# Two fused layer pairs on one core: separate q/k/v places for the first five chunks, a direct wo load, an instruction order planned from other costs, and down weights issued from GpSimd's queue

## The chip, the cores and the metric

The kernel runs on one core of a Trainium2 chip. The metric is device time in microseconds, as a median over runs of the whole program; the kernel before has 1096.06 (1095.94 to 1097.07, three runs). A separate profiled execution gives the trace from which all durations are read. TensorE does the matmuls, VectorE and ScalarE the elementwise work, GpSimd (POOL) set-up work, and SyncE (SP) issues the DMAs.

## The reference, cut to what matters

`x` is 2048 tokens by 576 channels. Attention has 32 heads of 18 channels, and each token looks at itself and at the tokens 2, 4, ... 14 before it.

```python
def A(x, wqkv, wo):                      # sliding, dilated attention
    q, k, v = split_heads(x @ wqkv)      # 576 -> 3 x 576
    idx = pos[:, None] - 2 * arange(8)   # 8 keys per token
    logits = sum_d(q * k[idx]) * Dh ** -0.5
    attn = softmax(where(idx >= 0, logits, -1e9))
    return merge_heads(sum_w(attn * v[idx])) @ wo
def B(x, w_gate, w_up, w_down):          # 576 -> 4608 -> 576
    return ((x @ w_gate) * (x @ w_up)) @ w_down

x = x + A(layernorm(x)); x = x + B(layernorm(x))
x = x + A(layernorm(x)); x = x + B(layernorm(x))
```

Both A layers share their weights, and so do both B layers.

## The kernel before, in words

**Chunks.** The tokens are cut into chunks, and a chunk goes through one A and one B before its x is kept in `xf`. The sequence `seq` holds 18 chunks, numbered j: for the first half of the tokens the first layer pair in chunks of 128, 128, 128, 128, 256 and 256 tokens (j = 0 to 5), then the second pair in four chunks of 256; then the second half of the tokens likewise in eight chunks of 256. A chunk needs the last 14 tokens of k and v of the chunk before it in its layer (the "halo").

**Attention of a chunk** (`attention`). `head` makes the layernorm: statistics on VectorE (L343, L344), rstd on ScalarE, nmr on VectorE (L352), and the normalized x on ScalarE (L358, with the last 64 channels a second time, L359). The transpose goes over TensorE (L369) and ScalarE (L372) for j below 5, by DMA (L362) otherwise. `project` multiplies with `wqkv` (L407) into the PSUM banks pg and pu, and ScalarE (for j = 0 partly VectorE) evacuates q, k and v into `qT`, `kT`, `vT` (L449 to L484). There are two sets of these places, and chunk j uses set j % 2: a projection can't be started before the chunk two before it has done its last product with v. Then VectorE multiplies q with shifted k (L503), adds (L507 to L512), TensorE sums over the channels (`Esel`, L518), VectorE and ScalarE do the softmax (L540 to L551). The weights of the softmax are spread to all channels: for j below 5 by TensorE (`Bsel`, L557) and copies (L447, L449), otherwise through DRAM, with one store (L567) and four loads `ab` (L570). VectorE multiplies with shifted v and adds up (L587, L602), in chunk 0 with TensorE adding (L591, L592). TensorE multiplies with `wo_p` (L614), VectorE adds x (L620), and a second `head` makes the input of B.

**B of a chunk** (`glu`). 36 slices of 128 hidden channels are done in units of 512 columns: gate and up by TensorE (L655, the last 64 channels as pairs of half matmuls, L666), ScalarE copies the gate out of PSUM (L677), VectorE multiplies (L678, `h`). After a phase of nine units (three for a chunk of 128 tokens), the "downs" multiply h with `wd` (L699, L700), and VectorE adds the sum to x (`settle`, L709, L714). Three PSUM pairs rotate among the units; a pair is free when its h is done.

**Down weights.** `load_wd` (L682) loads them in pieces of 288 KB into six buffers, issued by SyncE (324 loads). For a chunk of 256 tokens a phase has nine loads. They are recorded ahead of the downs of their phase, so the second load into a buffer waits for the landing of the first, and not for a down; the first three units of such a phase multiply with the weights of its last three. Both kernels do so.

**Start.** `wqkv` is loaded in five parts into `wraw`, and its columns are reordered by copies: columns t3 = 0 and 2 by VectorE (L292), 1 and 3 by ScalarE (L294). `setup_wo` loads wo into DRAM in the order of channels, then into `wo_p` (L320, L323). `setup_glu` loads gate and up in six slices; both stay in SBUF.

**Order.** Nothing is written out by hand. Every operation is recorded with an engine, a cost in ns, what it reads and writes, and a priority (`op`). `Plan.run` (L69) then simulates the engines with these costs: it takes again and again the operation that can start first, and emits it. The order so found is the order of each engine's instructions; the engines run in order, and so do the queues of SyncE and GpSimd. The PE work of B is one chain in fixed order (`bb`); matmuls of attention are put between.

Of the kernel before, what the change touches and what calls it, by code (L numbers as in the profile page):

```python
# [7 lines left out]
FP32 = mybir.dt.float32  # L8
# [7 lines left out]
class Op:  # L16
    __slots__ = ("eng", "cost", "fn", "deps", "order", "succ", "n", "prio", "idx", "hold", "free",
                 "lat", "margin", "ready", "end", "nbytes", "use", "pair", "need")


class Plan:
# [4 lines left out]
    LAT = {"PE": 250, "ACT": 130, "DVE": 110, "POOL": 150, "SP": 0}  # L26
# [6 lines left out]
    def op(self, eng, cost, fn, r=(), w=(), prio=1, after=None, hold=None, free=None, margin=0, nbytes=0, use=None,  # L33
           pair=None, need=None):
        o = Op()
        o.eng, o.cost, o.fn, o.prio, o.hold, o.free = eng, cost, fn, prio, hold, free
# [32 lines left out]
    def run(self, slots):  # L69
        clock = {e: 0.0 for e in self.LAT}  # L70
        dma = 0.0
# [3 lines left out]
        while cand:  # L75
            best = None
            for o in cand:
# [6 lines left out]
                if o.hold is not None:  # L84
                    f = free[o.hold]
                    if not f:
                        continue
                    t = max(t, min(f)[0])
                if o.pair is not None:
                    if len(free["unit"]) < len(o.pair):  # L90
                        continue
                    t = max(t, min(free["unit"])[0])
# [40 lines left out]
def kernel(  # L133
# [44 lines left out]
    wo_dram = dram.tile([D, D], BF16, name="wo_dram")  # L178
# [13 lines left out]
    xf = [sb(f"xf{i}", [P, NST, D], FP32) for i in range(NXS)]  # L192
# [9 lines left out]
    xnT_B = [sb(f"xnT_B{i}", [P, KT, CH]) for i in range(NXB)]  # L202
    qT_ = [sb(f"qT{i}", [P, KT, CH]) for i in range(2)]
    kT_ = [sb(f"kT{i}", [P, KT, HALO + CH]) for i in range(2)]
    vT_ = [sb(f"vT{i}", [P, KT, HALO + CH]) for i in range(2)]
    oT = sb("oT", [P, KT, CH])
    n_al = nlayers // 2
    halo_k = [sb(f"halo_k{i}", [P, KT, HALO]) for i in range(n_al)]
    halo_v = [sb(f"halo_v{i}", [P, KT, HALO]) for i in range(n_al)]
# [46 lines left out]
    def load_x(t0, nst):  # L256
        b, i0 = (t0 // 2) % 2, t0 % 2
        op("SP", 600, dma(xb[b][:, i0:i0 + nst, :], xv[:, t0:t0 + nst, :]), w=[f"xb{b}_{i}" for i in range(i0, i0 + nst)],
           nbytes=P * nst * D * 2, prio=1.5 if t0 else 0)
# [13 lines left out]
    def setup_b():  # L273
        def mk_zero():
            for t_ in qT_ + kT_ + vT_:
                nc.gpsimd.memset(t_[TL:P, KF, :], 0.0)
            for t_ in halo_k + halo_v:
                nc.gpsimd.memset(t_[:], 0.0)
        op("POOL", 1500, mk_zero, w=[f"{x}{t}{i}" for x in "qkv" for t in (4, "H") for i in range(2)] + [f"halo{x}{i}" for x in "kv" for i in range(n_al)])
        for k in range(KT):  # L280
            for t3 in (0, 1, 2, 3):
                if t3 < 3:
                    src = wraw[:, k, t3 * D:(t3 + 1) * D].rearrange("p (h d) -> p d h", h=H)[:, 0:16, :]
                    dst = wqkv[:, k, t3 * 512:(t3 + 1) * 512].rearrange("p (d h) -> p d h", h=H)
                    cost = (615, 1080)
                else:
                    src = wraw[:, k, :].rearrange("p (t h d) -> p t d h", t=3, h=H)[:, :, 16:18, :]
                    dst = wqkv[:, k, 3 * 512:3 * D].rearrange("p (t d h) -> p t d h", t=3, h=H)
                    cost = (280, 500)
                rk = [f"wraw{k}"] if k < KF else ["wrawt0", f"wrawt{TL}"]  # L290
                if t3 % 2 == 0:
                    op("DVE", cost[0], lambda dst=dst, src=src: nc.vector.tensor_copy(dst, src), r=rk, w=[f"wq{t3}_{k}"], prio=2)  # L292
                else:
# [10 lines left out]
        op("POOL", 9000, mk_sel, w=["sel"])  # L304
# [12 lines left out]
    def setup_wo():  # L317
        op("SP", 600, dma(wo_dram[:].rearrange("(d h) n -> h d n", h=H), A_wo.rearrange("(h d) n -> h d n", d=Dh)),
           w=["wod"], nbytes=D * D * 2, prio=2)
        op("SP", 600, lambda: nc.sync.dma_start(wo_p[:, 0:KF, :], wo_dram[0:KF * P, :].rearrange("(t p) n -> p t n", p=P)),  # L320
           r=["wod"], w=["wo0"], nbytes=KF * P * D * 2, prio=2)
        for r_ in (0, TL):
            op("SP", 600, lambda r_=r_: nc.sync.dma_start(wo_p[r_:r_ + TL, KF, :], wo_dram[KF * P:D, :]),  # L323
               r=["wod"], w=[f"wot{r_}"], nbytes=TL * D * 2, prio=2)
# [11 lines left out]
    def head(src, keys, nst, dst, key, prio, ab, on_pe, mg):  # L336

        mv, st, rstd, nmr, xn = mv_[ab], st_[ab], rstd_[ab], nmr_[ab], xn_[ab]
        for i in range(nst):
            def stats(i=i):  # L340
                xr = src(i).rearrange("p (a b) -> p a b", a=2)
                for a in range(2):
                    nc.vector.bn_stats(out=st[:, i, a, :], in_=xr[:, a, :])  # L343
                nc.vector.bn_aggr(out=mv[:, i, :], in_=st[:, i])  # L344
            op("DVE", 1070, stats, r=[keys[i]], w=[f"mv{ab}{i}"], prio=prio)
        mk = [f"mv{ab}{i}" for i in range(nst)]

        def rs():
            nc.scalar.activation(rstd[:, 0:nst], mv[:, 0:nst, 1], ACT.Ln, bias=eps_t[:])
            nc.scalar.activation(rstd[:, 0:nst], rstd[:, 0:nst], ACT.Exp, scale=-0.5)  # L350
        op("ACT", 490, rs, r=mk + ["eps"], w=[f"rstd{ab}"], prio=prio)
        op("DVE", 210, lambda: nc.vector.scalar_tensor_tensor(nmr[:, 0:nst], mv[:, 0:nst, 0], -1.0, rstd[:, 0:nst],  # L352
                                                              op0=ALU.mult, op1=ALU.mult),
           r=mk + [f"rstd{ab}"], w=[f"nmr{ab}"], prio=prio)
        for i in range(nst):
            def apply(i=i):
                x = src(i)
                nc.scalar.activation(xn[i][:, 0:D], x, ACT.Identity, bias=nmr[:, i:i + 1], scale=rstd[:, i:i + 1])  # L358
                nc.scalar.activation(xn[i][:, D:D + TL], x[:, KF * P:D], ACT.Identity, bias=nmr[:, i:i + 1], scale=rstd[:, i:i + 1])  # L359
            op("ACT", 1300, apply, r=[keys[i], f"nmr{ab}", f"rstd{ab}"], w=[f"xn{ab}{i}"], prio=prio)  # L360
            if not on_pe:
                op("SP", 900, lambda i=i: nc.sync.dma_start_transpose(out=dst[:, :, i * P:(i + 1) * P], in_=xn[i][:]),  # L362
                   r=[f"xn{ab}{i}"], w=[key + str(i)], prio=0, nbytes=P * KT * P * 2)
# [3 lines left out]
            def tr(i=i, b=b):  # L367
                for k in range(KT):
                    nc.tensor.transpose(bf(b())[:, k, :], xn[i][:, k * P:(k + 1) * P], ident[:])  # L369
            o = op("PE", 290, tr, r=[f"xn{ab}{i}", "ident"], prio=0, margin=mg, **b.take())  # L370
            pl.also(o, [key + str(i)])
            op("ACT", 700, lambda i=i, b=b: nc.scalar.copy(dst[:, :, i * P:(i + 1) * P], bf(b())), r=[b.key], w=[key + str(i)],  # L372
# [4 lines left out]

    def attention(j, la, t0, nst):
        fast = j == 0
        z = j % 2  # L380
        qT, kT, vT = qT_[z], kT_[z], vT_[z]
# [8 lines left out]
        xk = [f"xA{i}" for i in range(nst)]  # L390
        head(lambda i: xin[:, i0 + i, :], xin_k, nst, xnT_A, "xA", prio, 0, on_pe, mg)
        op("ACT", 250, lambda: nc.scalar.copy(kT[:, :, 0:HALO], halo_k[la][:]), r=[f"halok{la}"], w=[f"kH{z}"], prio=prio)
# [4 lines left out]
        def project(tag, au, bu, tl, ea, eb, dkeys):  # L397
# [7 lines left out]
            def mm(u, part, k, r_, start, stop):  # L405
                p_, e, c0, m = part
                nc.tensor.matmul(bank(p_, u)[0:m, e * n:(e + 1) * n], lhsT=wqkv[r_, k, c0:c0 + m], rhs=xnT_A[r_, k, 0:n],  # L407
# [387 lines left out]
```

## Time and profile before

| | |
|---|---|
| median of three runs | 1096.06 us |
| profiled execution | 1094.6 us |
| its span | 1092.5 us |
| VectorE busy, 200 to 600 us | 81% to 87% by 100 us |
| first gate matmul | at 43.20 us |
| DMA, 20 to 60 us, by 10 us | 319 to 347 GB/s |
| first load issued to its landing, down weights | median 3.4 us, 2.6 to 10.2 |

The span is one profiled execution from its first to its last instruction; 2.1 us of the profiled execution lie around it. A row of a timeline has the start, the length, the engine, the line of the kernel, the operation with output and inputs, and in brackets the idle time ahead of it with what ended it. PEld is TensorE's weight loading, which runs beside its matmuls. SPq is the issuing of DMAs on SyncE. A group's mean length can be longer than the pace of such operations in a row, since one begins before the last has quite ended.

### The profile page before, as it was taken

The numbers are of one execution on the slowest core, as the hardware profiler recorded it, in microseconds if no ns is written. First come the engines' busy times: TensorE is split into PE (matmuls) and PEld (weight loads), VectorE is DVE, ScalarE is ACT, GpSimd is POOL, SyncE is SP. The second block draws the span as 40 slices with busy tenths as digits, with TensorE's granted clock in tenths as the row PEclk, the third lists the DMA queues.
The fourth block names the chain that finished last, engine by engine and source line by source line (L and its number), as shares of the span: only waits on it lengthen the run. The fifth ranks groups of instructions, "written<-read, shape, count | busy, mean of one in ns | idle before, by whom it ended". The sixth has DMA issues, their size and how long they took to land.

```text
span 1092.5 us, 25296 instructions
## 1 busy us (share of the span) xinstructions
PE 1057.1 (97%) x10812; PEld 792.8 (73%) x10812; DVE 761.4 (70%) x1347; ACT 364.1 (33%) x768; POOL 5.9 (1%) x26
## 2 busy tenths in 40 slices
PE   5889999999999999999999899999999999999998
PEld 4668887777777777777767677777787777777775
DVE  6688889697979868798978563785757867322222
ACT  7435254432244443323342222314242232211111
POOL 2000000000000000000000000000000000000000
PEclk9899999999999999999999999999999999999999
DMA  8954563633333532535361434342333323333331
GB/s 261 336 155 119 172 200 98 183 110 97 95 99 102 147 84 74 135 112 155 99 168 24 122 99 122 92 121 56 117 106 122 107 72 121 105 96 109 116 110 55
DMA packets 146239, 133.17 MB, mean 122 GB/s; under 512 B 42000, under 2 KB 145488, under 8 KB 146128
## 3 DMA queue, kind: packets, MB, share of 16 engines
q1 hardware_dynamic: 146128, 131.57, 41.9%
q8 instruction: 84, 1.38, 0.5%
q14 instruction: 27, 0.22, 0.1%
HBM read 118.96 MB, written 4.73 MB: 113 GB/s over the span
## 4 chain that ended last, share of the span: by engine, by line
PE 88%; DVE 5%; DMA 4%; SPq 1%; issue 1%; ACT 1%; DVEq 0%; ACTq 0%
PE pu L655 21%; PE pg L655 21%; PE pg L699 12%; PE pu L699 10%; PE pg L666 6%; PE pg L407 6%; PE pu L407 4%; PE pa L614 3%; PE acct L700 3%; DMA a_dram<-s 2%; DMA ab<-a_dram 1%; SPq L570 1%; DMA wraw<-in_A_wqkv_dram 1%; DVE h L678 1%; DVE prod L503 1%
## 5 line engine op out<-in xcount | busy, mean ns | idle before, releaser
L677 ACT CAST g_sb<-pg 128x512 bf16<-128x512 f32 x288 | 158.9, 586 | 493.6 <-PE pu L666 359.7
L655 PE MATMUL pg<-xnT_B,wg 128*128 128x256 bf16 (+1 forms) x2592 | 301.1, 262 | 1.1 <-ACT xnT_B L372 1.1
L655 PE MATMUL pu<-xnT_B,wu 128*128 128x256 bf16 (+1 forms) x2592 | 301.9, 262 | 0.1
L678 DVE TENSOR_TENSOR h<-pu,g_sb 128x512 bf16<-128x512 f32 x288 | 193.3, 684 | 130.6 <-ACT g_sb L677 74.8
L655 PEld LDWEIGHTS <-wu 128*128 128x128 bf16 x2592 | 225.2, 98 | 40.1 <-issue 16.5
L655 PEld LDWEIGHTS <-wg 128*128 128x128 bf16 x2592 | 230.2, 98 | 28.9 <-issue 1.5
L699 PE MATMUL pg<-wd,h 128*128 128x512 bf16 x648 | 231.9, 382 | 0.0
L700 PE MATMUL acct<-wd,h 128*128 128x64 bf16 x1152 | 222.4, 193 | 0.0
L699 PEld LDWEIGHTS <-h 128*128 128x128 bf16 x1152 | 113.0, 98 | 130.5 <-issue 1.1
L699 PE MATMUL pu<-wd,h 128*128 128x512 bf16 x504 | 191.5, 380 | 0.9 <-DVE h L678 0.9
L587 DVE TENSOR_TENSOR prod<-vT,ab 128x1280 bf16<-128x1280 bf16 (+1 forms) x127 | 94.0, 741 | 47.1 <-DMA ab<-a_dram 46.0
L407 PEld LDWEIGHTS <-wqkv 128*128 128x128 bf16 (+1 forms) x1260 | 98.7, 99 | 25.6 <-issue 14.5
L700 PEld LDWEIGHTS <-h 128*128 128x128 bf16 x1152 | 113.1, 98 | 2.1 <-issue 1.1
L503 DVE TENSOR_TENSOR prod<-qT,kT 128x2560 bf16<-128x2560 bf16 (+1 forms) x72 | 95.7, 1332 | 22.4 <-ACT kT L449 21.9
L602 DVE TENSOR_TENSOR oT<-oT,prod 128x1280 bf16<-128x1280 bf16 (+1 forms) x119 | 90.8, 763 | 3.2
L666 PE MATMUL pu<-xnT_B,wgu_t 64*128 64x256 bf16 (+1 forms) x648 | 79.7, 259 | 4.2 <-DVE h L678 4.2
L407 PE MATMUL pg<-xnT_A,wqkv 128*128 128x256 bf16 (+3 forms) x650 | 79.7, 265 | 2.5 <-ACT xnT_A L372 1.6
L666 PE MATMUL pg<-xnT_B,wgu_t 64*128 64x256 bf16 (+1 forms) x648 | 79.8, 259 | 0.0
L407 PE MATMUL pu<-xnT_A,wqkv 128*128 128x256 bf16 (+3 forms) x610 | 77.2, 266 | 0.1
L709 DVE TENSOR_TENSOR xf<-pg,xf 128x512 f32<-128x512 f32 (+1 forms) x40 | 27.4, 684 | 66.3 <-PE pg L699 58.4
L666 PEld LDWEIGHTS <-wgu_t 64*128 64x128 bf16 x1296 | 50.3, 94 | 27.8 <-issue 22.6
L614 PE MATMUL pa<-wo_p,oT 128*128 128x288 bf16 x310 | 48.2, 286 | 2.5 <-DVE oT L602 1.8
(91 smaller groups left out, 614.0 us busy)
## 6 DMA issues: line engine op xcount, KB each, us to landing
wd<-in_B_w_down_dram SPq DMA_DIRECT2D x324, 288.0 KB, 3.4
ab<-a_dram SPq DMA_DIRECT2D x52, 128.0 KB, 2.7
wg<-in_B_w_gate_dram SPq DMA_DIRECT2D x6, 768.0 KB, 9.4
wu<-in_B_w_up_dram SPq DMA_DIRECT2D x6, 768.0 KB, 10.7
out_dram<-xf SPq DMA_DIRECT2D x8, 288.0 KB, 5.4
wraw<-in_A_wqkv_dram SPq DMA_DIRECT2D x4, 432.0 KB, 5.5
xb<-in_A_x_dram SPq DMA_DIRECT2D x6, 288.0 KB, 4.6
a_dram<-s SPq DMA_DIRECT2D x13, 128.0 KB, 2.2
```

The costliest lines, as they stand in the source:

```text
L407: nc.tensor.matmul(bank(p_, u)[0:m, e * n:(e + 1) * n], lhsT=wqkv[r_, k, c0:c0 + m], rhs=xnT_A[r_, k, 0:n], start=start, stop=stop, skip_g ...
L503: nc.vector.tensor_tensor(late["prod"][p_ % 2][:, :, :, 0:n], q2, k2, op=ALU.mult)
L587: nc.vector.tensor_tensor(js(dst), js(vT[:, :, o0:o0 + n]), abw, op=ALU.mult)
L602: op("DVE", 60 + 3 * n, lambda i_=i_: nc.vector.tensor_tensor(oT[:, :, 0:n], oT[:, :, 0:n], late["prod"][i_ % 2][:, 0, :, 0:n], op=ALU.add ...
L614: nc.tensor.matmul(b()[:, 0:HD], lhsT=oT[:, t, i * P:(i + 1) * P], rhs=wo_p[:, t, hh * HD:(hh + 1) * HD], start=(t == 0), stop=(t == KT - 1))
L655: nc.tensor.matmul(pt[:, e * n:(e + 1) * n], lhsT=w_[:, k, ft * P:(ft + 1) * P], rhs=xT[:, k, 0:n], start=(first and k == 0 and e == 0), s ...
L666: nc.tensor.matmul(ps[:, e * n:(e + 1) * n], lhsT=wgu_t[r_, ft * P:(ft + 1) * P], rhs=xT[r_, KF, 0:n], start=(first and e == 0), stop=not ...
L677: op("ACT", 590, lambda: nc.scalar.copy(g_sb[gs][:, 0:ul], pg[use["slot"]][:, 0:ul]), r=[f"wg_{j}_{u}"], w=[f"g{gs}"], prio=0)
L678: op("DVE", 690, lambda: nc.vector.tensor_tensor(hb[hs][:, 0:ul], pu[use["slot"]][:, 0:ul], g_sb[gs][:, 0:ul], op=ALU.mult), r=[f"wu_{j}_{ ...
L699: nc.tensor.matmul((pg, pu)[i][use["slot"]][:], lhsT=lhs, rhs=wt[:, e % 2, 0:512], start=first, stop=fin)
L700: nc.tensor.matmul(acct[:, i * TL:(i + 1) * TL], lhsT=lhs, rhs=wt[:, e % 2, 512:D], start=(first and i == 0), stop=fin, skip_group_check=True)
L709: op("DVE", 690, lambda i=i, dst=dst: nc.vector.tensor_tensor(dst[:, 0:512], (pg, pu)[i][use["slot"]][:], xs_f[:, i0 + i, 0:512], op=ALU.add),
```

## The change

- Chunks 0 to 4 get places of their own for q, k and v: the two sets are cut in halves for the four chunks of 128, and chunk 4 uses memory of `xf` (buffers 2 and 3) that is not needed yet. k and v lie in one tile, so that the halo takes one copy instead of two each way.
- Chunk 4's x is loaded a second time, early, into a part of `xf` (`xtmp`), and its first layernorm is recorded with chunk 3.
- wo goes from its input to `wo_p` directly, in six loads.
- A third of the copies that reorder `wqkv` goes to GpSimd; VectorE and ScalarE divide the others anew. GpSimd also clears the new places.
- For j below 5, L359 is left out and the transposes of the last 64 channels take their place (12 more on TensorE); for chunks of 128 tokens the softmax weights are spread in two copies instead of four.
- Nearly all costs in the recorded operations are different, most of them lower. The model of DMAs has a queue for GpSimd and some extra latency (`late`). Gate copies and h are marked `due`: an operation that isn't due is put off if it would delay one that is by more than a slack.
- All loads of down weights but the first six are issued by GpSimd.

In the built order the counts of matmuls by line are unchanged but for the 12 transposes. The projections of chunks 2 and 3 stand ahead of the first gate matmul, and chunk 4's stands in the first phase of chunk 0's B. SyncE issues 178 DMAs, transposes included, instead of 493, GpSimd 318 instead of none.

```diff
 class Plan:
-    LAT = {"PE": 250, "ACT": 130, "DVE": 110, "POOL": 150, "SP": 0}
+    LAT = {"PE": 250, "ACT": 150, "DVE": 150, "POOL": 150, "SP": 0}
...
+                if o.due and (o.eng not in urgent or key < urgent[o.eng][0]):
+                    urgent[o.eng] = (key, o)
+            o = best[1]
+            if not o.due and o.eng in urgent and urgent[o.eng][0][0] < best[0][0] + o.cost - SLACK[o.eng]:
+                best = urgent[o.eng]
...
-                dma = max(dma, o.end) + o.nbytes / 250.0
-                o.ready = dma + 2000
+                dma[o.eng] = max(dma[o.eng], o.end) + o.nbytes / (250.0 if o.eng == "SP" else 200.0)
+                o.ready = dma[o.eng] + 2000 + o.late
...
-                if t3 % 2 == 0:
+                if t3 == 0 or t3 == 3:
                     op("DVE", cost[0], lambda dst=dst, src=src: nc.vector.tensor_copy(dst, src), ...)
+                elif t3 == 2:
+                    op("POOL", 1000, lambda dst=dst, src=src: nc.gpsimd.tensor_copy(dst, src), ...)
...
     def setup_wo():
-        op("SP", 600, dma(wo_dram[:].rearrange("(d h) n -> h d n", h=H), A_wo.rearrange("(h d) n -> h d n", d=Dh)), ...)
-        op("SP", 600, lambda: nc.sync.dma_start(wo_p[:, 0:KF, :], wo_dram[0:KF * P, :].rearrange("(t p) n -> p t n", p=P)), ...)
+        wv_ = A_wo.rearrange("(h d) n -> h d n", d=Dh)
+        for dd in range(4):
+            op("SP", 470, dma(wo_p[32 * dd:32 * dd + 32, 0:KF, :], wv_[:, dd:16:4, :]), ...)
...
+    def place(j, nst):
+        if nst == 1:
+            z, h = j // 2, j % 2
+            return [2 * z + h], qT_[z][:, :, h * P:h * P + P], kv_[z][:, :, :, h * (HALO + P):(h + 1) * (HALO + P)], h * P
+        if j == 4:
+            return ["x"], q_x, kv_x, 0
+        z = (j + 1) % 2
+        return [2 * z, 2 * z + 1], qT_[z][:], kv_[z][:, :, :, 0:HALO + CH], 0
...
-        z = j % 2
-        qT, kT, vT = qT_[z], kT_[z], vT_[z]
+        zs, qT, kv, c0 = place(j, nst)
+        kT, vT = kv[:, 0], kv[:, 1]
...
-            op("ACT", 590, lambda: nc.scalar.copy(g_sb[gs][:, 0:ul], pg[use["slot"]][:, 0:ul]), ..., prio=0)
-            op("DVE", 690, lambda: nc.vector.tensor_tensor(hb[hs][:, 0:ul], ...), ..., prio=0, free="unit", use=use)
+            op("ACT", 490, lambda: nc.scalar.copy(g_sb[gs][:, 0:ul], pg[use["slot"]][:, 0:ul]), ..., prio=0, due=True)
+            op("DVE", 605, lambda: nc.vector.tensor_tensor(hb[hs][:, 0:ul], ...), ..., prio=0, due=True, free="unit", use=use)
...
-            op("SP", 550, dma(wd[b][:], wd_v[g]), ...)
+            first = wd_no["n"] <= NWD
+            eng, q = ("SP", nc.sync) if first else ("POOL", nc.gpsimd)
+            op(eng, 550 if first else 1100, lambda: q.dma_start(wd[b][:], wd_v[g]), ..., late=0 if first else 1000, ...)
```

More of the change, by code (lines that the diff above doesn't have):

```diff
@@ L17 @@
     __slots__ = ("eng", "cost", "fn", "deps", "order", "succ", "n", "prio", "idx", "hold", "free",
-                 "lat", "margin", "ready", "end", "nbytes", "use", "pair", "need")
+                 "lat", "margin", "ready", "end", "nbytes", "use", "pair", "need", "due", "late")
+SLACK = {"DVE": 500, "ACT": 300}
 class Plan:
-    LAT = {"PE": 250, "ACT": 130, "DVE": 110, "POOL": 150, "SP": 0}
+    LAT = {"PE": 250, "ACT": 150, "DVE": 150, "POOL": 150, "SP": 0}
     def __init__(self):
@@ L351, in head @@
[L351 to L354, printed above, removed]
+                    nc.vector.bn_stats(out=st[:, ia + i, a, :], in_=xr[:, a, :])
+                nc.vector.bn_aggr(out=mv[:, ia + i, :], in_=st[:, ia + i])
@@ L488, in attention @@
[L488 to L491 removed]
+            ev_t += [(270, lambda u, d: cp(d, kT[0:TL, KF, HALO:HALO + n], bank(0, u)[TL:P, 0:n]), zk("k4"), 1),
+                     (270, lambda u, d: cp(d, vT[0:TL, KF, HALO:HALO + n], bank(1, u)[TL:P, 0:n]), zk("v4"), 0)]
@@ L493, in wv @@
+        op("ACT", 150, lambda: nc.scalar.copy(halo[la][:], kv[:, :, :, n:n + HALO]),
+           r=zk("k0", "k2", "k4", "v0", "v2", "v4"), w=hk, prio=prio)
+        if j == 3:
+            head(lambda i: xtmp[:, i, :], ["xt0", "xt1"], NST, xnT_A, "xA", prio, 0, on_pe, mg)
+        qk = zk("q0", "q2", "q4", "k0", "k2", "k4", "kH")
         def wv(t):
@@ L757 @@
     for j, (l, t0, nst) in enumerate(seq):
-        if l == 0 and j:
+        if l == 0 and j >= 4:
             load_x(t0, nst)
```

226 lines of the change are left out of this document (127 added, 99 removed).

## The prediction

> **What bounds the kernel.** I read the page's busy table first, then stages of 10 us, then the waits ahead of TensorE in its timeline, then the queue of SyncE.
>
> ```profile
> PE 1057.1 (97%) x10812; PEld 792.8 (73%) x10812; DVE 761.4 (70%) x1347; ACT 364.1 (33%) x768; POOL 5.9 (1%) x26
> ```
>
> TensorE is busy all but 35.4 of 1092.5 us. The change leaves its work alone: matmul counts by line are equal (5184 gate/up, 1152 + 1152 down, 1260 projections), but for 12 more transposes. So only waits can go, and matmuls at the low clock. The stages (window, then busy us of PE, PEld, DVE, ACT, POOL, then clock) say where the waits are:
>
> ```profile
> 0.00:10.00 10.00, 1.95 (x18) 1.79 (x19) 4.61 (x11) 7.61 (x13) 5.87 (x26) 1.00 0.80 242
> 10.00:20.00 10.00, 6.02 (x109) 5.25 (x108) 7.54 (x17) 8.55 (x21) 0.00 (x0) 0.96 0.71 210
> 20.00:30.00 10.00, 6.96 (x120) 5.77 (x117) 6.25 (x22) 6.54 (x19) 0.00 (x0) 0.84 1.07 347
> 40.00:50.00 10.00, 7.37 (x118) 6.78 (x119) 5.20 (x15) 5.24 (x14) 0.00 (x0) 0.83 1.07 338
> 60.00:70.00 10.00, 7.53 (x111) 6.10 (x109) 9.31 (x21) 3.49 (x10) 0.00 (x0) 1.00 0.15 49
> 70.00:80.00 10.00, 7.01 (x87) 4.96 (x86) 8.25 (x24) 3.70 (x9) 0.00 (x0) 0.83 0.70 206
> ```
>
> The idle in 0 to 80 us sums to 24.0 (80 less 56.0 busy), 4.1 lie at 610 to 630, 4.3 in the closing stage 1080 to 1092, and some 2.4 in six short waits between 200 and 914. TensorE's timeline (start, length, [wait <- releaser]):
>
> ```profile
> 19.65 1.89 PE L407 MATMUL pg<-xnT_A,wqkv 128*128 128x128 bf16 x16
> 60.91 1.06 PE L407 MATMUL pg<-xnT_A,wqkv 128*128 128x128 bf16 x16
> 64.71 0.79 PE L614 MATMUL pa<-wo_p,oT 128*128 128x288 bf16 x5 [1.85 <-DVE oT L602]
> 73.62 0.21 PE L518 MATMUL pa<-s,Esel 128*32 128x64 bf16 x4 [2.50 <-DVE s L512]
> 622.41 0.27 PE L666 MATMUL pu<-xnT_B,wgu_t 64*128 64x256 bf16 x1 [4.08 <-DVE h L678]
> ```
>
> The first two rows are the same 16 matmuls: after a wait they take 1.89 us instead of 1.06, so a long wait costs more than its length. The wait at 622 comes out of SyncE's queue, which issues in order (SyncE's timeline, then VectorE's, then SyncE's waits in total, times, longest):
>
> ```profile
> 603.79 6.09 SPq L250 DMA_DIRECT2D wd<-in_B_w_down_dram  x6
> 610.45 0.46 SPq L567 DMA_DIRECT2D a_dram<-s  x1
> 620.94 0.83 DVE L587 TENSOR_TENSOR prod<-vT,ab 128x1280 bf16<-128x1280 bf16 x1 [6.82 <-DMA ab<-a_dram]
> ...
> SPq L250 <- PE acct L700: 333.7, 57, 22.7
> SPq L250 <- DMA wd<-in_B_w_down_dram: 192.6, 81, 4.2
> ```
>
> The softmax result was ready at 606.5; its store stood behind six loads of down weights until 610.45, landed after 5.39 us (median 2.2), and VectorE sat before the first product with the h of the next unit behind it.
>
> **Part 1: start to the first gate matmul.** Before, that is at 43.20 us. The built order puts the projections of chunks 2 and 3 ahead of it; before, chunk 2's stood there (34.12 us, after chunk 0's last product, whose q/k/v place it reuses) and chunk 3's at 60.91. That moves 70 matmuls, 3.5 us warm (1.06 + 1.06 less overlap, tails, 1.27 and 0.61), plus one transpose into time that was idle.
>
> Does 43.20 itself move? Chunk 0's projection ends at 14.4 now. GpSimd takes five of the weight copies. It must first clear two new places and wo's tail: 1.4 us more, from its memsets (0.32 for 270 elements, 0.52 for 512), so it is free near 8.0 instead of 6.6. Its copy of 128x512 is in no row: at least VectorE's 0.61, at most ScalarE's 1.1. I take 0.8, nearer VectorE. And these rows of GpSimd show a stretch beside VectorE's weight copies (at 4.31 and 4.94, 0.6 each):
>
> ```profile
> 4.36 0.64 POOL L300 TENSOR_SCALAR_AFFINE_SELECT Esel<-Esel 128x32 bf16<-128x32 bf16 x1
> 4.96 0.76 POOL L302 TENSOR_SCALAR_AFFINE_SELECT Bsel<-Bsel 128x128 bf16<-128x128 bf16 x1
> 5.68 0.21 POOL L300 TENSOR_SCALAR_AFFINE_SELECT Esel<-Esel 128x32 bf16<-128x32 bf16 x1
> 5.84 0.31 POOL L302 TENSOR_SCALAR_AFFINE_SELECT Bsel<-Bsel 128x128 bf16<-128x128 bf16 x1
> ```
>
> Each lost 0.44. With copies taking turns this way, the five end near 15, and the projection near 15.9 (bounds: 14.4 at 0.61 without turns, 17.3 at 1.1 with). VectorE hides most of it: before, it evacuated k only at 16.28, behind two layernorm statistics, and now at 16.0. Then the chain runs as before: products, two more statistics (2.0 us for chunk 4, half under the sums on TensorE), softmax, its spread in two copies instead of four (0.5 less), eight products whose sums now stand between parts of chunk 2's projection (about 1 more), wo, layernorm without L359 (0.42 less). I get 43.0, between 42.3 and 44.5. TensorE is then 3.9 us further: **-4** (bounds -5 and -2.3).
>
> wo's load has no second step. SyncE stood 6.7 us for it before wo_p's (15.07); the gate weights go out two to three us sooner, and nothing waited for them. No gain. The merged halo, k/v and softmax copies save ScalarE about 0.5 us a chunk; it is 33% busy: nothing.
>
> **Part 2: 43 to 90 us.** Here chunk 4's projection (0.98 per 8 matmuls of 256, 6.6 in all) now follows the first units, since it has a place of its own and its x was fetched early. It fills TensorE while VectorE does chunk 1's softmax. Gone are 2.47 + 2.99 idle and 1.4 of low clock (six down matmuls at 0.61 against 0.38, from 73.77). What is late next is wo of chunk 1: by rows, its products (15 x 0.49) start once both spreads are copied, near 56, and end near 63.5, just when TensorE has done two more units. I leave 1.4 us of new waits (0 to 4): **-5.5**.
>
> **Part 3: the steady part.** SyncE loses 318 of its 324 down loads. At 603.79 the store would go at once, 3.9 us sooner, and not share the engines with six loads. The h operations are also marked due, so that a product waiting for a DMA isn't put ahead of them. The wait of 4.08 and its low clock after it (1.33 + 1.71 + 1.35 against 0.98 each) go: **-5.5**. The other 2.4 I leave.
>
> The order is now made from lower costs (VectorE's h 605 instead of 690; a row's mean is 684, but two in a row take 1.28). That is true to the pace, but it takes away cover that the old, high costs gave. VectorE is 81 to 87% busy from 200 to 600, so a product chain that comes 1 us late finds less slack. I book **+2** for it, bounds 0 and 8, since no row shows such an order.
>
> **Part 4: loads on GpSimd's queue.** No row shows one. They don't wait for the downs of their own phase (a second load of a buffer waits for the first's landing), so the row to scale is the last phase's: nine issues from 1055.68 to 1067.1, that is three landings of 3.05 and five issues of 0.45. With landing L and issue i the ninth lands 4L + 5i after 1055.6, and its unit multiplies at 1083.8. With SyncE's i TensorE waits from L = 6.5 on, with twice that from 5.9; I reckon with 5.9. The nearest rows for L are SyncE's landings, 2.6 to 10.2, median 3.4. A shorter one would gain nothing, since TensorE waits for no load now. I take 3.9, the median and one more issue: **0**; the upper end is the first rival. Behind a waiting load stand only other loads.
>
> **Sum.** 1094.6 (the profiled execution: span 1092.5 and 2.1 around it) - 4 - 5.5 - 5.5 + 2 = 1081.6. The median of the runs shown, 1096.06, is 1.5 above it: **1083.0**. With all bounds: 1076 (-5, -6.9, -7.9, 0) to 1093 (-2.3, -2.9, -5.5, +8).
>
> **Against it, from the skill.** The Trainium skill's DMA: Bandwidth & Descriptors (Issuing engines are not separate DMA queues) says that issuing from several engines saves only issue time. By that rule part 3's 5.5 would stay, and the time be 1088.5. The rows at 603.79 and 610.45 speak of waits in the issuing queue, not of bandwidth, so I keep my sum and give that case 10 of the forecast's 73%, in whose range it lies.
>
> **Rivals.**
> - Loads starve (slower). GpSimd's 0.44 us stretches show that VectorE can hold it up, and VectorE is busy 70%. If each load lands at L = 7.2, twice the median and some, the four phases of the last two chunks wait 4 x 1.3 each (21 us), and the other 24, with half a chunk's attention work between them (half of a projection's 6.6 and wo's 2.4, so 4.5), 0.7 each (17): 1121. It decides from L = 6.7, where 16 x 0.8 eats the gain. Against it: the stretching operations were copies; the steady ones are two-input products. The Trainium skill, SBUF — State Buffer (Who interferes with whom), has some copies hold the port pair that GpSimd's descriptor writing needs, and infers that two-input operations leave it free. By that rule L stays short; no run here shows it yet. 9%.
> - The tight order (slower). If a third of the fourteen 256-token chunks each meet one wait like the one at 622 (5.5), that is 26 in place of 2: 1107. For it: the old order made six waits with loose costs. Against: h goes first now. 8%.
> - The gain is lost again (no change): projection 0 ends at 17.3 (-2.3), wo of chunk 1 is late by 4 (-2.9), another wait takes the place of 622's (0) and 5 us of short ones come: 1096. 8%.
> - The forecast, 1076 to 1093: 73%. Below it: 2%.
>
> A measurement tells 0.2%, 2.2 us, from no change. Faster 0.75, same 0.08, slower 0.17. The range runs from 1076 to 1099: it takes in the no-change case and leaves out 2% below and nearly all of the 17% above.
>
> **What would show it.** Right: PE idle in 0 to 80 us down from 24 to some 15, with the first gate matmul at 42.3 to 44.5; no wait of TensorE above 2 us between 90 and 1080; down loads landing under 5.9 us. Wrong: TensorE waiting for down weights, GpSimd's copies ending after 17, or h waiting behind products again.

## The result, and the profile after

The changed kernel takes 1114.59 us (median of four runs, 1110.56 to 1117.24) against 1096.0 for the kernel before beside it: a ratio of 1.0169 (95% interval 1.0148 to 1.0190). It is slower by 1.7%, where I had forecast 1.2% faster, and outside my range. The profiled execution took 1110.56 us, its span is 1108.7.

The busy line of the page after, and the first stages (the same columns as before):

```profile
PE 1058.9 (96%) x10752; PEld 793.9 (72%) x10824; DVE 760.4 (69%) x1346; ACT 352.9 (32%) x704; POOL 242.7 (22%) x348
```

```profile
0.00:10.00 10.00, 2.62 (x22) 2.09 (x23) 5.81 (x13) 7.25 (x10) 9.15 (x27) 1.00 0.83 262
10.00:20.00 10.00, 7.07 (x123) 6.10 (x122) 8.67 (x20) 6.07 (x16) 4.17 (x4) 0.89 1.08 310
20.00:30.00 10.00, 8.35 (x119) 7.20 (x115) 7.27 (x26) 6.64 (x15) 0.00 (x0) 0.77 1.07 349
40.00:50.00 10.00, 9.21 (x177) 8.46 (x177) 7.04 (x17) 7.22 (x15) 0.00 (x0) 1.00 1.07 330
60.00:70.00 10.00, 9.95 (x152) 8.31 (x152) 9.76 (x23) 1.66 (x3) 4.04 (x7) 1.00 0.53 179
70.00:80.00 10.00, 9.95 (x166) 8.03 (x166) 7.95 (x21) 4.13 (x8) 4.22 (x6) 1.00 0.63 209
```

Up to 80 us the change does what I said: every stage shown has more TensorE work, and the idle time falls from 24.0 to 13.8. The loss is behind that. TensorE's timeline after, the first gate matmul and four of the longest waits:

```profile
43.16 1.05 PE L709 MATMUL pg<-xnT_B,wg 128*128 128x128 bf16 x16 [0.79 <-ACT xnT_B L399]
...
203.80 0.27 PE L720 MATMUL pu<-xnT_B,wgu_t 64*128 64x256 bf16 x1 [1.99 <-DVE h L732]
...
257.98 0.59 PE L756 MATMUL pu<-wd,h 128*128 128x512 bf16 x1 [5.57 <-DVE h L732]
...
309.94 1.03 PE L709 MATMUL pu<-xnT_B,wu 128*128 128x256 bf16 x8 [3.53 <-DVE h L732]
...
608.66 1.86 PE L709 MATMUL pu<-xnT_B,wu 128*128 128x256 bf16 x8 [2.70 <-DVE h L732]
```

The last four wait for h, as the one at 622 us did. Summed over the timeline, TensorE's waits behind 80 us grow from 6.5 us (5.1 for h) to 26.6 (16.8 for h): 20.1 more, against 10.2 won ahead of 80. The span grows by 16.2. What is left, some 6 us, is mostly matmuls at the low clock behind long waits, such as the last row's: 1.86 us for eight that take 1.03 in the row above. The granted clock was 0.65 to 0.84 in 25 us after (255 to 265, 310 to 315 and 605 to 615) and 0.83 in 10 us before (620 to 630); from these clocks I estimate some 5 us more lost. (I use these waits, and not the idle time of the windows, since 72 down matmuls are missing from the records after: 10752 matmuls to 10824 weight loads.)

Why h is late at 257.98 takes three queues, after. First GpSimd's, then SyncE's, then VectorE's timeline:

```profile
228.72 0.72 POOL L741 DMA_DIRECT2D wd<-in_B_w_down_dram  x1 [33.49 <-PE acct L757]
...
233.62 2.16 POOL L741 DMA_DIRECT2D wd<-in_B_w_down_dram  x3 [0.26 <-PE acct L757]
236.96 0.72 POOL L741 DMA_DIRECT2D wd<-in_B_w_down_dram  x1 [1.18 <-DMA wd<-in_B_w_down_dram]
```

```profile
231.66 3.67 SPq L387 DMA_TRANSPOSE xnT_B<-xn  x2
241.20 0.36 SPq L621 DMA_DIRECT2D a_dram<-s  x1
249.90 1.75 SPq L624 DMA_DIRECT2D ab<-a_dram  x4
```

```profile
246.17 0.69 DVE L732 TENSOR_TENSOR h<-pu,g_sb 128x512 bf16<-128x512 f32 x1 [1.05 <-PE pu L709]
254.17 0.83 DVE L641 TENSOR_TENSOR oT<-kv,ab 128x1280 bf16<-128x1280 bf16 x1 [7.32 <-DMA ab<-a_dram]
...
257.25 1.28 DVE L732 TENSOR_TENSOR h<-pu,g_sb 128x512 bf16<-128x512 f32 x2
```

As the downs free the buffers, nine loads of 288 KB go out between 228.72 and 237.68. The store of the softmax is issued at 241.20 and lands only at 249.9, 8.7 us later (median 1.7). Ahead of it in SyncE's queue are no loads, but the two transposes issued from 231.66 on. They land late too, the second 12.6 us after its issue (median of all transposes 2.7), near 246.0. The two of this stretch, shortest, median and longest:

```profile
DMA to landing us min/median/max: 8.0/10.3/12.6
```

So the reload `ab` is late, VectorE sits 7.32 us before the first product, and the next h stands behind it.

### The profile page after: what moved, and what is told of

The parts are those of the page before. It is cut to its first block, busy times and chain, and to the rows that moved or that the text cites. A ratio compares the mean times of both kernels' runs of the same rounds, so it can differ in the third digit from the quotient of the medians.

```text
span 1108.7 us, 25201 instructions
## 1 busy us (share of the span) xinstructions
PE 1058.9 (96%) x10752; PEld 793.9 (72%) x10824; DVE 760.4 (69%) x1346; ACT 352.9 (32%) x704; POOL 242.7 (22%) x348
## 2 busy tenths in 40 slices
DMA packets 84848, 132.74 MB, mean 120 GB/s; under 512 B 42048, under 2 KB 63744, under 8 KB 84736
## 3 DMA queue, kind: packets, MB, share of 16 engines
q0 software_dynamic: 25440, 93.80, 28.4%
## 4 chain that ended last, share of the span: by engine, by line
PE 72%; DVE 16%; DMA 7%; issue 2%; ACT 1%; SPq 1%; POOL 0%; DVEq 0%; POOLq 0%; ACTq 0%
PE pu L709 18%; PE pg L709 18%; PE pg L756 9%; PE pu L756 7%; PE pg L720 5%; PE pg L455 5%; PE pu L455 3%; DVE prod L641 3%; PE pa L668 3%; PE acct L757 3%; DVE oT L655 3%; DMA ab<-a_dram 3%; DMA a_dram<-s 2%; DVE h L732 2%; DVE prod L553 2%
## 5 line engine op out<-in xcount | busy, mean ns | idle before, releaser
L741 POOL DMA_DIRECT2D wd<-in_B_w_down_dram x318 | 229.4, 723 | 836.2 <-PE acct L757 800.2
L756 PE MATMUL pg<-wd,h 128*128 128x512 bf16 x605 | 218.0, 382 | 0.1
L756 PE MATMUL pu<-wd,h 128*128 128x512 bf16 x475 | 181.9, 383 | 6.7 <-DVE h L732 6.7
L553 DVE TENSOR_TENSOR prod<-qT,kv 128x2560 bf16<-128x2560 bf16 (+1 forms) x68 | 90.0, 1326 | 24.3 <-ACT kv L497 23.3
L641 DVE TENSOR_TENSOR prod<-kv,ab 128x1280 bf16<-128x1280 bf16 (+1 forms) x120 | 88.3, 738 | 2.1 <-PE pg L646 1.9
```

The source lines that it names most:

```text
L553: nc.vector.tensor_tensor(late["prod"][p_ % 2][:, :, :, 0:n], q2, k2, op=ALU.mult)
L641: nc.vector.tensor_tensor(js(dst), js(vT[:, :, o0:o0 + n]), abw, op=ALU.mult)
L741: op(eng, 550 if first else 1100, lambda: q.dma_start(wd[b][:], wd_v[g]), w=[f"wd{b}"], nbytes=P * 2 * D * 2, late=0 if first else 1000, p ...
L756: nc.tensor.matmul((pg, pu)[i][use["slot"]][:], lhsT=lhs, rhs=wt[:, e % 2, 0:512], start=first, stop=fin)
```

## The experiments

My theories. **A, the flood:** GpSimd's loads go out in bursts and get in the way of store and reload. **B, the tight order:** the new order puts products, with h behind them, too near, loads or no loads. **C, the blind plan** (added after the first four runs): the new planner gives GpSimd's queue a DMA clock of its own (`dma[o.eng]`), so it plans store and reload as if the loads weren't there.

Waits are TensorE's behind 80 us, those for h in brackets; ratios are to the kernel before, run on the same chip, whose median was 1094.6 to 1097.1 us from set to set. In the orders of e4, e5, e7, e10, e12 and e13 one chunk's layernorm scale is overwritten before it is read; the amount of work is the same, so they stand for the time alone. (The text of e13 counts TensorE's idle time of the windows instead, in which the closing stage and missing records are included.)

| run | time, us | ratio (95%) | waits, us |
|---|---|---|---|
| before / changed | 1096.0 / 1114.6 | 1.0169 (1.0148 to 1.0190) | 6.5 (5.1) / 26.6 (16.8) |
| e1_thin_loads | 1083.4 | 0.9892 (0.9871 to 0.9913) | 6.6 (0) |
| e8_half_loads | 1089.7 | 0.9962 (0.9945 to 0.9979) | 12.0 (4.3) |
| e2_sync_loads | 1099.2 | 1.0045 (1.0025 to 1.0064) | 14.3 (6.5) |
| e3_before_pool | 1098.6 | 1.0039 (1.0018 to 1.0060) | 9.4 (4.7) |
| e4_late | 1089.5 | 0.9930 (0.9901 to 0.9958) | 12.0 (1.1) |
| e5_one_dma | 1102.4 | 1.0082 (1.0053 to 1.0110) | 14.0 (0.6) |
| e7_nodue | 1115.9 | 1.0192 (1.0170 to 1.0214) | 28.6 (14.1) |
| e10_both_late | 1090.0 | 0.9958 (0.9940 to 0.9976) | 10.9 (1.8) |
| e12_one_dma_later | 1090.0 | 0.9946 (0.9929 to 0.9962) | 13.2 (3.1) |
| e9_same_order_sync | 1095.7 | 1.0009 (0.9997 to 1.0021) | 15.7 (8.2) |
| e14_same_order_act | 1101.3 | 1.0059 (1.0038 to 1.0080) | 20.3 (10.1) |
| e15_before_order_pool | 1112.7 | 1.0161 (1.0133 to 1.0190) | 22.7 (13.4) |
| e11_before_thin | 1085.3 | 0.9908 (0.9893 to 0.9923) | 1.2 (0) |
| e13_sync_late | 1081.8 | 0.9886 (0.9862 to 0.9910) | 5.3 (0) |
| e16_sync_late_rstd | 1083.0 | 0.9878 (0.9861 to 0.9896) | 6.2 (0.3) |

**Is it the bytes?** The order is the changed kernel's; only the size of the loads is less.

```diff
-lambda: q.dma_start(wd[b][:], wd_v[g])
+lambda: q.dma_start(wd[b][:], wd_v[g]) if first else q.dma_start(wd[b][0:16], wd_v[g][0:16])   # e8: 0:64
```

> The changed kernel with every down-weight load behind the first six cut to 16 of its 128 partitions (36 KB in place of 288 KB), so the rest of each tile keeps the first six tiles' weights: part of the down weights is left out. The order on every engine, each wait and the number of loads stay. Theory A, the flood: GpSimd's queue holds nothing but these loads, so nine of them (2.65 MB) go out back to back as the downs free the buffers, and the store of the softmax and its four reloads share the 16 DMA engines with them (store landing up to 8.7 us, reload 7.0 us); VectorE stands at the first product with h behind it, and TensorE waits for h. Then here the store lands in 2 us each time, store to first product is 8 us at most in all 13 chunks (measured 6.0 to 13.0), the waits for h between 200 and 620 fall from 16.7 us to under 3, and the time is 1085 to 1097 us. Theory B, the tight order: the new order itself puts the products too near; then the waits stay, and the time is 1104 to 1117.

> The changed kernel with every down-weight load behind the first six cut to 64 of its 128 partitions (144 KB), the other half of each tile keeping the first six tiles' weights: part of the down weights is left out; order and waits stay. It measures how the time goes with the bytes: 288 KB gave 1110 to 1117 us, 36 KB 1083. If the loss goes with the bytes of the burst, 1093 to 1102; if there is a point below which the store and reload get through in time (their planned 6.7 us), 1083 to 1089; if the number of GpSimd's issues mattered and not the bytes, 1083 for 36 KB would not have come out.

With thin loads no h is waited for, and the time is even 1.6 us under A's range. That it is also my forecast to 0.4 us is luck: the forecast had the whole loads in it. A holds and B falls as the cause of these waits (one store to product was still 9.26 us, over the 8 that A allowed). Half the bytes cost 6 to 7 us, all of them some 30: neither in proportion, nor nothing below a point.

**Loads back on SyncE, and one part alone in the old kernel.**

```diff
-            first = wd_no["n"] <= NWD          # e2, in the changed kernel
+            first = True
...
-            op("SP", 550, dma(wd[b][:], wd_v[g]), ...)          # e3, in the kernel before
+            first = wd_no["n"] <= NWD
+            eng, q = ("SP", nc.sync) if first else ("POOL", nc.gpsimd)
+            op(eng, 550 if first else 1100, lambda: q.dma_start(wd[b][:], wd_v[g]), ...)
```

> The changed kernel with all down-weight loads back on SyncE's queue and planned there, at the cost that the first six have (550 ns, nothing added to the landing); all else of the change stays, and the order is made anew with these costs. Theory A, the flood: SyncE's queue is in order and the store is put ahead of the loads, so the store lands in 2 to 5 us as before the change, VectorE's waits for the reload with h behind it go, and the time is 1083 to 1097 us. Theory B, the tight order: the waits for h stay at 10 us or more, and the time is 1104 to 1117.

> The kernel before with one part of the change alone: the down-weight loads behind the first six are issued by GpSimd, planned at 1100 ns each on that engine; the old costs and rules of the order stay. Theory A, the flood: the loads now go out in bursts of nine beside the store and its reloads, store to first product grows past 11 us in several chunks (11.8 at most before), and the time is 1101 to 1116 us against 1096. Theory B, the tight order: the loads' queue is worth nothing by itself or a little gain (the store no longer stands behind loads at 622 us), 1090 to 1099.

Neither fits A alone. e2 lies between the theories: the order, made anew, lost 4.6 us of the startup (idle to 80 us 18.4). In e3 GpSimd's queue cost only 0.4%. What both share, and the changed kernel lacks, is one DMA clock for all loads: their planners had put the products 9 to 11 us behind the store where nine loads go out, the changed one 6.7. Hence C.

**Telling the planner.**

```diff
-r=[f"adr{j % 2}", "ab"], w=[f"ab{g}"], prio=0, nbytes=P * W * sq * 2, late=1200)
+r=[f"adr{j % 2}", "ab"], w=[f"ab{g}"], prio=0, nbytes=P * W * sq * 2, late=5200)     # e4
...
-late=3000)     # the transposes
+late=6000)     # e10, with e4's edit
...
-dma[o.eng] = max(dma[o.eng], o.end) + ...
+dma["SP"] = max(dma["SP"], o.end) + ...     # e5; e12: only where o.end >= 90000
...
-SLACK = {"DVE": 500, "ACT": 300}
+SLACK = {"DVE": 10**6, "ACT": 10**6}     # e7
```

> The changed kernel with one number of the order's model changed: the reload of the softmax is planned to land 5.2 us late in place of 1.2, so that the products are planned 13.2 us behind the store, as far as the longest measured (13.0). The loads stay on GpSimd. By theory A, the flood, the landings stay long (store up to 8 us, reload 7), but h now goes ahead of the products, so most of the 16.7 us of waits for h goes and only waits for what follows the products (the output projection) can take their place: 1088 to 1103 us. By theory B, the tight order, this is the whole cure: 1083 to 1093. If the time stays at 1104 or more, h behind the waiting product is not how the time is lost.

> The changed kernel, planned with one DMA clock for both queues instead of one each; loads, queues and everything else as changed. The planner has the store and first product 6.7 us apart in nine of the first nine-load stretches although up to twelve loads go out beside them; measured were 11 to 13. With one clock it plans 9.5 to 13.4 us there. Theory C, the blind plan: the split DMA clock is the part of the change that turned the flood into lost time, since it lets the order put products (and h behind them) where the reload can't be. Then the waits for h between 200 and 620 fall from 16.7 to under 6 us and the time is 1084 to 1098 us (the shared clock delays some work too much). Rival, the rule that puts h first or the shaved costs made the order brittle, whatever the clocks: 1102 to 1115.

> The changed kernel with the planner's rule off by which h and the gate copies go ahead of other work (slack so large that it never applies); the two DMA clocks, the costs and GpSimd's loads stay. Store to first product is again planned at 6.7 to 7.8 us beside up to nine loads. Theory C, the blind plan: this changes little, waits for h stay at 8 us or more, 1100 to 1117 us. Rival, the rule is what made the order brittle: 1083 to 1096. My prediction's part 3, that the rule is what keeps h from standing behind the products, would make it slower than the changed kernel, 1113 to 1122.

> The changed kernel, planned with the reload of the softmax landing 5.2 us late (1.2 as changed) and each DMA transpose 6.0 us late (3.0 as changed); GpSimd's loads, the two clocks and the rule for h stay. With the reload's number alone the time was 1089.5 us, and TensorE still waited 1.9 and 2.6 us for transposed activations behind the loads. Theory C, the blind plan: with both landings told to the planner TensorE waits under 8 us in all behind 80 us, and the time is 1079 to 1089 us, below both kernels. If the bursts cost time in another way than by what the plan does not know of them, it stays at 1088 or more.

> The changed kernel, planned with one DMA clock for both queues as soon as the planned time is past 90 us, and with one each before that. With one clock from the start the time was 1102 us, but 4.2 us of its loss was a wait at 74 us, with low clock behind it, that the shared clock had put into the startup (60 us of TensorE work before 80 us, 66 in the changed kernel); the waits for h behind the reload were gone. Here the startup is the changed kernel's. Theory C, the blind plan: store to first product is planned at 9.9 to 13.0 us where nine loads go out, waits for h stay under 4 us, TensorE works 408 us or more between 200 and 620 (396 in the changed kernel, 417 in the kernel before), and the time is 1083 to 1096 us. If sharing the clock only moves the loss to other waits, it is 1098 or more.

With the loads still on GpSimd, a planner that knows of late reloads gets back some 25 us (e4, e12). e4's time lies in the ranges of A and B alike; that its stores and reloads still took up to 7.8 and 6.9 us to land speaks for A. (In e4 the planner's own times put the product 10.7 us behind the store, and not 13.2, as I had reckoned; 6.7 without the edit.) e5 took the waits for h away too (0.6), but its time is in the rival's range: the shared clock spoiled the startup (idle to 80 us 20.2). e12 leaves the startup alone, and C holds. e10 came out 1 us above its range, on the side of "another way", and TensorE still waited 10.9 us: the transposes' number gives nothing more, so C is not the whole loss. e7's time fits C and my part 3 alike, but its interval overlaps that of the changed kernel, and the waits for h are there with the rule (16.8 us) and without it (14.1): the rule for h neither made the harm nor cures it.

**The queue itself.** e9 and e14 keep the changed order to the instruction and move only the issue; e15 does so in the old order.

```diff
-lambda: q.dma_start(wd[b][:], wd_v[g])     # e9, changed kernel; e14: (q if first else nc.scalar)
+lambda: nc.sync.dma_start(wd[b][:], wd_v[g])
...
-dma(wd[b][:], wd_v[g])     # e15, kernel before
+dma(wd[b][:], wd_v[g]) if wd_no["n"] <= NWD else lambda: nc.gpsimd.dma_start(wd[b][:], wd_v[g])
...
+thin = slice(0, P if wd_no["n"] <= NWD else 16)     # e11, kernel before
-dma(wd[b][:], wd_v[g])
+dma(wd[b][thin], wd_v[g][thin])
```

> The changed kernel with every down-weight load issued by SyncE, but planned as if GpSimd issued it: the order on TensorE, VectorE and ScalarE is the changed kernel's, instruction for instruction, and only the queue is another. It tells the queue from the moment of the burst. If what hurts is that nine loads of 288 KB go out when store and reload are due, whichever queue they are in, the store lands behind them here too (in SyncE's own queue, or standing behind a load that waits for its buffer): 1100 to 1120 us, VectorE waiting for the reload in the chunks at 200 to 360. If GpSimd's queue itself is what slows SyncE's transfers, the same order gives 1083 to 1095 here.

> The changed kernel with every down-weight load behind the first six issued by ScalarE, in the planned place of GpSimd's: the order of all other work is the changed kernel's. A third place for the same burst: GpSimd's queue gave 1114.6 us, SyncE's 1095.7. If any second queue beside SyncE's lets the loads into the way of the transposes, the store and the reload, 1105 to 1120. If GpSimd's queue alone does it (its packets are of 3.7 KB, SyncE's loads are cut to about 1.1 KB), 1090 to 1102. A cost that belongs to neither: each issue takes ScalarE's time (0.39 us on SyncE), and a load that waits for its buffer holds the gate copies behind it; up to 8 us of TensorE waits for gate copies would be that, and are to be taken off.

> The kernel before with its order untouched to the instruction on TensorE, VectorE and ScalarE; only the issue of the down-weight loads behind the first six goes to GpSimd. It fills the table of two orders and two queues: old order with SyncE 1094.9 us, new order with SyncE 1095.7, new order with GpSimd 1114.6. If GpSimd's queue costs the same in any order that does not plan for it, 1108 to 1116. If the old order has the room to take it, 1095 to 1103 (planned anew for GpSimd it was 1098.6).

> The kernel before, its order and queues untouched, with every down-weight load behind the first six cut to 16 of its 128 partitions (36 KB), so part of the down weights is left out. With the changed kernel's 1083.4 us at the same cut it says what the rest of the change is worth without the loads in the way, and what the loads cost the old order. My prediction had 9.5 us of gain before 90 us (parts 1 and 2), and 4.1 us of wait at 622 with its low clock behind it, which thin loads take away: 1088 to 1092 us. If the old order stood the loads at no cost but that at 622, 1090; if the loads cost the old order 10 us or more, 1080 to 1085, and then the new order's own gain is nothing.

| | thin loads | SyncE | ScalarE | GpSimd |
|---|---|---|---|---|
| old order | 1085.3 | 1094.9 | | 1112.7 |
| new order | 1083.4 | 1095.7 | 1101.3 | 1114.6 |
| new order, reload planned later (e16, e4) | | 1083.0 | | 1089.5 |

e9 came 0.7 us above the range for "the queue itself", e14 into that for "GpSimd's queue alone", e15 into its first. e11 is in none of its ranges: the loads cost the old order 9.6 us, where I had only the wait at 622.

This corrected A: it isn't the moment of the burst but its queue. GpSimd's costs some 18 us over SyncE's in either order, ScalarE's 6 (none of TensorE's waits there ends with a gate copy, and VectorE waits for gate copies 86 us in all, 87 in e9, so ScalarE's own time isn't the reason). B comes back in a weaker form. With the loads in SyncE's queue the new order still waits 8.2 us for h. Even with thin loads it is worth only 1.9 us (1085.3 less 1083.4): TensorE idles 7.0 us less before 80 us, and waits 5.4 us more behind it, mostly at the output projection. The DMA engines' busy tenths and GB/s around the same burst (windows of 40 us, 1 us a column), in the changed kernel:

```profile
DMA  0000499999679979592598500199000000000000
GB/s 0 0 0 0 46 304 340 295 263 125 40 143 155 102 209 172 48 110 74 195 331 303 198 2 1 19 265 229 10 0 0 0 0 0 0 0 0 0 0 0
...
wd<-in_B_w_down_dram POOLq DMA_DIRECT2D x10, 288.0 KB, 8.5
...
a_dram<-s SPq DMA_DIRECT2D x1, 128.0 KB, 8.7
xnT_B<-xn SPq DMA_TRANSPOSE x2, 10.3
```

and with the same order and SyncE's queue (e9), two rows of SyncE's timeline first:

```profile
232.72 2.58 SPq L741 DMA_DIRECT2D wd<-in_B_w_down_dram  x5
238.25 0.34 SPq L621 DMA_DIRECT2D a_dram<-s  x1
...
DMA  0000389997898999840891000000000077989999
GB/s 0 0 0 0 37 262 372 356 268 35 215 286 189 294 307 351 308 146 5 253 249 26 8 0 0 0 0 0 0 0 0 0 188 197 303 235 312 292 220 304
...
a_dram<-s SPq DMA_DIRECT2D x1, 128.0 KB, 1.8
xnT_B<-xn SPq DMA_TRANSPOSE x2, 4.2
```

and with ScalarE's queue (e14):

```profile
DMA  0000499999917999999502970000000004899839
GB/s 0 0 0 0 106 339 243 315 297 262 108 7 124 180 300 160 196 298 321 187 7 62 285 177 0 0 0 0 0 0 0 0 0 98 226 268 289 253 103 297
...
a_dram<-s SPq DMA_DIRECT2D x1, 128.0 KB, 4.4
xnT_B<-xn SPq DMA_TRANSPOSE x2, 9.4
```

In e9 the nine loads stand around the two transposes in one queue and are nearly over when the store comes. In the changed kernel they run beside the transposes: in the eleventh to the nineteenth column the engines are busy mostly by half or more, but move only 40 to 209 GB/s, the transposes take 10.3 us instead of 4.2, and the store stands behind the second of them and falls into the rest of the burst. Both seem to count: of the 13 stores the slowest two, 8.7 and 6.9 us, went out with a transpose and five or six loads in flight; one with five loads and no transpose in flight took 4.5. In e14 the transposes take nearly as long (9.4), but the burst is over sooner and the store takes 4.4. The longest landing of a transpose is 5.4 us with SyncE's queue, 10.2 with ScalarE's, 12.6 with GpSimd's; that of a store 4.4, 5.3 and 8.7.

**Both cures.**

```diff
-lambda: q.dma_start(wd[b][:], wd_v[g])
+lambda: nc.sync.dma_start(wd[b][:], wd_v[g])
...
-w=[f"ab{g}"], ..., late=1200)
+w=[f"ab{g}"], ..., late=5200)
...
-r=[keys[i], nk[i]], w=[f"xn{ab}{ia + i}"]
+r=[keys[i], nk[i], rk[i]], w=[f"xn{ab}{ia + i}"]     # e16 alone
```

> The changed kernel with two edits: the loads issued by SyncE (planned as if GpSimd issued them), and the reload planned to land 5.2 us late in place of 1.2. With the first edit alone the time was 1095.7 us and TensorE stood idle 20.7 us behind 80 us, against 11.4 in the kernel before and 36.0 in the changed one; with the second alone 1089.5. If the rest of the loss is the products planned too near the reload, the idle time behind 80 us falls to 8 to 13 us and the time to 1083 to 1089. If the two edits cure the same thing, 1088 to 1092. If the new order loses its gain in some other way, 1093 or more.

> The changed kernel with three edits: down-weight loads issued by SyncE in the places planned for GpSimd, the reload planned to land 5.2 us late in place of 1.2, and the planner told that the normalization reads the scale that the two small activations ahead of it write (in the orders of e4_late, e5_one_dma, e7_nodue, e10_both_late, e12_one_dma_later and e13_sync_late the scale of one 256-token chunk, rows 1024 to 1279 in the second attention layer, had been overwritten by the next chunk's before it was read; the work was the same). With the first two edits the time was 1081.8 us. The third moves a few of ScalarE's instructions in one place and nothing on the other engines, so 1080.5 to 1084 us, 1.0 to 1.4% below the kernel before. Were the two causes not the whole loss, the time would not stay under my forecast for the changed kernel, 1083.0, by more than that.

e13 came out 1.2 us below its range, e16 is in its own. e16 is the best version that keeps every scale: 0.9878 of the kernel before (e13's 0.9886 is the same within the intervals). That this is the 1.2% I had forecast for the changed kernel is no confirmation, since it took two more edits to get there. The longest wait of TensorE behind 80 us in e16:

```profile
384.33 0.24 PE L568 MATMUL pa<-s,Esel 128*32 128x128 bf16 x4 [1.47 <-DVE s L562]
```

## Why the prediction was wrong

- **Part 1, right.** The projections of chunks 2 and 3 stand ahead of the first gate matmul, and that is at 43.16 us (forecast 43.0). GpSimd's copies end at 14.2 (near 15), though one alone takes 1.10 us, my upper bound: beside VectorE's copies only two of the five were stretched, to 1.51. In 43.0 there is some luck: VectorE evacuated k at 14.89, 1.4 us sooner than before and not 0.3 as I had it, and the products with v then lost that again (1.57 us of wait for TensorE at 31.68).
- **Part 2, right.** Idle to 80 us went down by 10.2; parts 1 and 2 had 9.5 with 1.4 of low clock in it. Between 43.16 and 90 us TensorE waits for nothing now, where I had left 1.4 us of new waits.
- **Part 3, wrong.** "h first", by the mark `due`, was to end waits like the one at 622. With the mark off the time is much the same (e7: 1.0192 of the kernel before, against 1.0169 with it). And "tight order +2, bounds 0 and 8" was far too small: with the loads on SyncE the new order's waits behind 80 us are 15.7 instead of 6.5, so 9.2 more where I had 3.5 less. That gives the startup's gain back (1095.7 against 1094.9). The order plans 6.7 us from store to product; planned 4 us later, 5.3 to 6.2 us of waits are left (e13, e16). But the distance alone doesn't tell the orders apart, since the old plan has 5.5 to 8.1 us there; which of the new costs and rules made the order so sensitive was not tested apart and stays open.
- **Part 4, wrong, and the largest miss.** I asked whether TensorE would wait for down weights. It never did, with a median landing of 4.5 us (threshold 5.9; longest 12.3). I did not ask who else is on the DMA engines while nine loads go out. That term was 0 and measured 18.9 (1114.6 less e9's 1095.7; 17.8 with each taken against the kernel before of its own runs). In its place the runs showed that the loads, in a queue beside SyncE's, slow the transposes, the store and the reload, and with them the first product and h.
- **The rivals.** "Tight order" (1107, 8%) was nearest in what one sees, waits like 622's in chunk after chunk. But the whole new order, low costs included, makes only 1095.7 without GpSimd's queue. "The gain is lost again" has the time of e9, though not by its steps. "Loads starve" did not come: GpSimd's issues took 0.72 us each, 0.84 at most, beside a busy VectorE.

The Trainium skill's DMA: Bandwidth & Descriptors (Issuing engines are not separate DMA queues) says that issuing from several engines saves only issue time. I gave that case 10 of the 73%, and my 0 in part 4 took no more than an issue from the change of queue. The runs agree that all queues share the DMA engines and that transfers interleave, but not with the rest: one order, three queues, 1095.7, 1101.3 and 1114.6 us. Another section of that page (Queues, rings and completion order) says that a DMA engine takes its queues in turn, a packet each. The loads had packets of 3.69 KB on GpSimd's queue (93.80 MB in 25440) and 1.08 KB on ScalarE's (93.80 MB in 86496), and 42048 packets of the rest are under 512 B. By that rule, if its packets are the ones counted here, large packets take most of the time from small ones, which fits the order of the three times. It doesn't fit all: the total falls to 40 GB/s and less while loads and transposes are in flight together, and ScalarE's small packets hold up the transposes nearly as long as GpSimd's large ones. No run here shows the turns themselves, so why the queues slow each other stays open, and the packet size is an argued cause at most.

## What to carry to other kernels

When DMAs move to another queue, list what is in flight beside them, not only who waits for them: a queue in order also keeps bulk loads and short urgent transfers apart, as e9 did here. The planner that gave each queue its own DMA clock put work where its data couldn't be yet; plan the landing measured beside the burst. Cutting the bytes of a suspected transfer at an unchanged order (e1) separates contention from order in one run.

## What the runs showed of the hardware

- The same loads in the same order cost some 12 us over thin ones on SyncE's queue (1095.7 against 1083.4), 18 on ScalarE's, 30 on GpSimd's, each taken against the kernel before of its own runs.
- A DMA transpose that lands in 2.7 us at the median took up to 5.4 us with the loads in its own queue, 10.2 with them in ScalarE's and 12.6 in GpSimd's.
- The old order pays 9.6 us for its loads on SyncE (1094.9 less 1085.3).
- Five 128x512 copies on GpSimd beside VectorE's took 1.09 to 1.51 us each. In the steady part GpSimd's issues left VectorE alone: h took 685 ns with them and 684 before.
